# An adaLN transformer block on one core: another order of the opening, with the diagonals of silu(c) on ScalarE and all sixteen modulation columns on VectorE

## The chip, the cores and the metric

The kernel runs on one core of a Trainium2 chip. The metric is the device time of one execution in microseconds, given as the median of the runs. A core has five engines that run at the same time, each with its own in-order instruction stream: TensorE (PE in the profile, its weight loads PEld), VectorE (DVE), ScalarE (ACT), GpSimd (POOL) and SyncE (SP), which here issues the DMA transfers.

## The reference

A row `c` modulates a transformer block of two parts; everything is float32.

```python
mod = (silu(c) @ w_mod).reshape(1, 6, 1, 1024)      # sa, ca, ga, sb, cb, gb
h = layernorm(x) * (1 + ca) + sa                    # x: 2048 x 1024
x = x + ga * A(h)       # attention over 4 segments of 512 rows, 32 heads of 32,
                        # o = g * (memory of earlier segments) + (1 - g) * softmax attention, g = sigmoid(beta)
h = layernorm(x) * (1 + cb) + sb
x = x + gb * ((gelu(h @ w_gate) * (h @ w_up)) @ w_down)
```

Before any projection of the first segment of attention can start, the first two sixths of `mod` are needed (`sa` and `ca`): 2 x 1024 numbers, each a dot product of silu(c) with a column of `w_mod`.

## The kernel before, in words

The kernel has an opening, the attention stage and the feed-forward stage. The change touches the opening alone. In it the order of the instructions on each of the five engines is the order in which the program issues them: the string `OPENING` is read token by token, and each token issues a few instructions on one or several engines. An instruction at the head of an engine's queue that waits holds up all that was issued to that engine after it.

What the opening does, with the names of the profile:

- **Modulation columns.** A tile `wm` holds 128 columns of `w_mod`, turned so that each partition holds one column of 1024 numbers. `mod_col` (L175) multiplies it on VectorE by silu(c), repeated on all partitions in `scp`, and sums into one column of `modT`; for the scales (1 + ca) a second instruction adds one (L180). Block `kt` of the first segment needs the columns `C<kt>` (scale, number 8 + kt) and `c<kt>` (shift, number kt). The 16 tiles are loaded in eight pairs into four buffers of two halves (`wm_a` to `wm_d`), so that pairs 4 to 7 (tokens `p4` to `p7`) wait until the columns of pairs 0 to 3 are done. Two columns, `c6` and `C7`, are made on PE instead (`mod_mm`, L186): 16 matmuls each with one output column, and ScalarE copies the result (L187).
- **The silu row.** `scol` is silu(c) as 1024 numbers on 128 partitions. `row_parts` (L140) makes two tiles of diagonals on VectorE, one matmul with a tile of ones each (L146) puts the row on all partitions (`scp`), and ScalarE copies it to `scb` (L147), which the later columns use.
- **Normalization.** For each of four tiles of 128 rows: statistics on VectorE (L236 to L241; `s0` to `s3` for the first segment, `t0` to `t3` for the second), a power on GpSimd (L242), one small factor on VectorE (L1900) and two scalings by halves on ScalarE (L1903; `a0` to `a7`, `b0` to `b3`).
- **Blocks of h.** `norm_seg` (`n` for the first segment, `N` for the second): four transposes of x on PE (L350), which read one half of all four tiles; then ScalarE applies the columns (L357, `h`) and rounds to the high part (L363, `hha`), and GpSimd subtracts to the low part (L368, `hla`); in the second segment some of these two run on VectorE. The call that finishes block kt issues the transposes of block kt + 1.
- **Weights.** `rk`, `rq` and `rv` of the first head group are split in the same way: ScalarE rounds (`K`, first `q`, first `v`), and the rest is subtracted on VectorE (k, L194) or in four quarters on GpSimd (q and v, L204).
- **Projections.** `F` calls `first_part`: for each of eight blocks, twelve matmuls for keys and values (L590) and three for queries (L593); the ninth `F` copies keys and values out (`kn`, `vx`), the tenth turns the keys (`kT`), splits queries and keys (L469, L473, L443, L444) and sends them by DMA. `K` in the attention stage is the same for the second segment.
- **Beside these.** `selectors` makes a few small constant tiles; the gate shares `gall` (sigmoid of beta) and `omc` are made on ScalarE and VectorE (L131 to L133, L1888); two instructions on ScalarE spread a selector over 32 partitions of `ks` (L1906), all of this ahead of the first token. `x0` to `x3` load the second segment's x tiles into four buffers, three of which have held `rk`, `rq` and `rv`. `S` closes the opening's PSUM pool and opens the next.

Of the kernel before, what the change touches and what calls it, by code (L numbers as in the profile page):

```python
# [19 lines left out]
P = 128  # L20
D = 1024
# [15 lines left out]
def block_kernel(ctx: ExitStack, tc: tile.TileContext, x, c, wmod, wq, wkv, wo, beta, wg, wu, wd, out):  # L37
# [51 lines left out]
    def tmp_tile(name):  # L89
        return big.tile([P, L], F32, name=name, tag="tmp", bufs=4)  # L90
# [11 lines left out]
    def s_ps(name):  # L102
        return small[0].tile([P, L], F32, name=name, tag="s", bufs=small[2])
# [17 lines left out]
    ccol = cs([P, KT], "ccol")  # L121
    nc.sync.dma_start(ccol, c)
    bb = cs([P, H], "bb")
    nc.sync.dma_start(bb, bass.AP(tensor=beta.tensor, offset=beta.offset, ap=[[0, P], [1, H]]))
    def fetch(src, name):
        r = raw_tile("r" + name)
        nc.sync.dma_start(r, src)
# [7 lines left out]
    def row_parts(dst, cols, tmp, name):  # L135

        dgs = []
        for h in range(2):
            dg = tmp(f"{name}dg{h}")
            nc.vector.tensor_tensor(dg.rearrange("p (k m) -> p k m", m=P), ident.unsqueeze(1).to_broadcast([P, 4, P]),  # L140
                                    cols[:, 4 * h:4 * h + 4].unsqueeze(2).to_broadcast([P, 4, P]), op=ALU.mult)
            dgs.append(dg)
        yield
        for h in range(2):
            ps = scp[:, h * L:(h + 1) * L] if name == "sc" else s_ps(f"{name}{h}")
            nc.tensor.matmul(ps, ones, dgs[h], start=True, stop=True)  # L146
            nc.scalar.activation(dst[:, h * L:(h + 1) * L], ps, AF.Copy)  # L147
            yield
# [25 lines left out]
    def mod_col(r, w, behind=False):  # L174
# [3 lines left out]
            hold(i)  # L178
        if r // 8 in (1, 4):
            nc.vector.tensor_scalar_add(modT[:, r:r + 1], modT[:, r:r + 1], 1.0)  # L180

    def mod_mm(r, w):

        ps = s_ps(f"col{r}")
        for k in range(KT):
            nc.tensor.matmul(ps[:, :1], w[:, k * P:(k + 1) * P], scol[:, k:k + 1], start=(k == 0), stop=(k == KT - 1))  # L186
        nc.scalar.activation(modT[:, r:r + 1], ps[:, :1], AF.Identity, bias=1.0 if r // 8 == 1 else 0.0)  # L187

    def split_w(r, w, eng=nc.gpsimd):
        nc.scalar.activation(w[:, 0], r, AF.Copy)
# [698 lines left out]
    def feed_forward():  # L891
# [946 lines left out]
    AFTER = ('qo kt ek dq ea dk eb', 'kt qo ea eb dk dq ek')  # L1838
    HI_DVE = ((), (1, 5, 7))
    LO_DVE = ((), (0, 1, 5, 6, 7))  # L1840
    BY_PRODUCT = (6, 15)
    OPENING = (
        "s0 s1 a2 r r s2 a5 r q s3 a6 a4 a0 c0 C1 C0 K q n n a3 v p4 c1 q q C2 c3 c2 n p5 v C4 C3 F c5 n F q "
        "c4 F x0 v p6 p7 v a7 a1 C5 n v x1 t0 C6 n n F x2 c6 n x3 C7 c7 b0 t1 t2 F F n b1 F t3 F b2 S b3 F F "
        "N N N N N ")

    def opening():
        x0 = [[], []]
        for i in range(4):
            for h in range(2):  # L1850
                tag, bufs = ("pt0", 4) if h == 0 else ("sj", 3) if i < 3 else ("pq", 2)
                t = t2(f"x0_{i}_{h}", tag, bufs=bufs)
                nc.sync.dma_start(t, x[i * P:(i + 1) * P, h * L:(h + 1) * L])
                x0[h].append(t)
        free = [wsp_tile("wm_a"), wsp_tile("wm_b")] + [
            t2(f"wm_{q}", "qs", bufs=2, dt=F32R, shape=(P, 4, L)).rearrange("p (a b) t -> p a (b t)", a=2) for q in "cd"]
        spare = [f32(w[:, h]) for w in free for h in range(2)]
        got, raw0, x1t, x1h = {}, {}, [], [[], []]

        def pair(kt):  # L1860
            for r in (8 + kt, kt):
                got[r] = mod_load(r, spare[len(got) % 8])

        def x1_load(i):
            x1t.append(fetch(x[L + i * P:L + (i + 1) * P, :], f"x1_{i}"))

        pair(0)
        raw0[1] = fetch(wkv[0, 0], "k0")
        raw0[0] = fetch(wq[0], "q0")
        pair(1)  # L1870
        raw0[2] = fetch(wkv[0, 1], "v0")
        pair(2)
        pair(3)

        nc.vector.memset(ones, 1.0)
        nc.gpsimd.affine_select(ident, ones, pattern=[[-1, P]], compare_op=ALU.is_equal, fill=0.0,
                                base=0, channel_multiplier=1)
        nc.vector.memset(mask, 0.0)
        nc.gpsimd.affine_select(mask[:, L - P:], mask[:, L - P:], pattern=[[-1, P]],
                                compare_op=ALU.is_ge, fill=MASK, base=0, channel_multiplier=1)  # L1880
        nc.vector.memset(mhalf, -0.5)
        selectors()
        sigmoid(scol, ccol)
        nc.vector.tensor_mul(scol, scol, ccol)
        sigmoid(gall, bb)
        for j in range(4):
            q = slice(DH * j, DH * (j + 1))
            nc.vector.tensor_scalar(omc[q], gall[q].rearrange("p (g j) -> p g j", j=4)[:, :, j], -1.0, 1.0,  # L1888
                                    op0=ALU.mult, op1=ALU.add)
        row = row_parts(scb, scol, tmp_tile, "sc")  # L1890
        sc = {}

        def stats(s, i, halves):
            sc[s, i] = norm_stats([halves[h][i] for h in range(2)], f"a{s}_{i}") + ([],)

        def scaled(s, i, hs, halves):
            mv, rs, mr = sc[s, i]
            if not mr:
                mr.append(cs([P, 1], f"mr{s}_{i}", tag="mr", bufs=4))
                nc.vector.tensor_scalar(mr[0], mv[:, 0:1], rs, -1.0, op0=ALU.mult, op1=ALU.mult)  # L1900
            for h in hs:
                t = halves[h][i]
                nc.scalar.activation(t, t, AF.Identity, bias=mr[0], scale=rs)  # L1903

        for k in ks_t:
            nc.scalar.activation(k[96:128], selj[96:128].unsqueeze(2).to_broadcast([32, 4, L]), AF.Copy)  # L1906
        W[0] = [wsp_tile(f"w0_{i}") for i in range(3)]
        nseg = norm_seg(0, x0)
        low = [split_parts(raw0[i], W[0][i]) for i in range(3)]
        first, nseg1 = [], []  # L1910
        for u in OPENING.split():
            n = int(u[1:]) if u[1:] else 0
            if u[0] == "p":
                pair(n)
            elif u[0] == "x":
                x1_load(n)
                for h in range(2):
                    x1h[h].append(x1t[n][:, h * L:(h + 1) * L])
            elif u[0] == "r":
                next(row)  # L1920
            elif u[0] in "st":
                stats("st".index(u[0]), n, (x0, x1h)[u[0] == "t"])
            elif u[0] == "a":
                scaled(0, n // 2, (n % 2,), x0)
            elif u[0] == "b":
                scaled(1, n, (0, 1), x1h)
            elif u[0] == "C":
                (mod_mm if 8 + n in BY_PRODUCT else mod_col)(*got[8 + n])
            elif u[0] == "c":
                (mod_mm if n in BY_PRODUCT else mod_col)(*got[n])  # L1930
            elif u[0] == "K":
                split_w(raw0[1], W[0][1], nc.vector)
            elif u[0] in "qv":
                next(low["q.v".index(u[0])])
            elif u[0] == "n":
                next(nseg)
            elif u[0] == "N":
                if not nseg1:
                    nseg1.append(norm_seg(1, x1h))
                next(nseg1[0])  # L1940
            elif u[0] == "F":
                if not first:
                    first.append(first_part(0, 0, 0))
                next(first[0])
            elif u[0] == "S":
                s_all()
        return nseg1[0]
# [73 lines left out]
    def selectors():  # L2021
        pick = tmp_tile("pick")[:, :P].rearrange("p (j d) -> p j d", d=DH)
        nc.gpsimd.affine_select(pick, ones.rearrange("p (j d) -> p j d", d=DH), pattern=[[-1, 4], [-4, DH]],
                                compare_op=ALU.is_equal, fill=0.0, base=0, channel_multiplier=1)
        nc.vector.tensor_reduce(sel4, pick, axis=AX.X, op=ALU.add)
        nc.vector.tensor_copy(blk.rearrange("p (j e) -> p j e", e=DH), sel4.unsqueeze(2).to_broadcast([P, 4, DH]))
        eye = tmp_tile("eye")[:, :32].rearrange("p (j i l) -> p j i l", j=4, i=4)
        nc.gpsimd.affine_select(eye, ones[:, :32].rearrange("p (j i l) -> p j i l", j=4, i=4),
                                pattern=[[-8, 4], [-2, 4], [-1, 2]], compare_op=ALU.is_equal, fill=0.0,
                                base=-96, channel_multiplier=1)  # L2030
        nc.vector.tensor_reduce(selj, eye.rearrange("p j i l -> p j (i l)"), axis=AX.X, op=ALU.add)
        nc.vector.tensor_copy(seli, eye[:, 0, :, 0])
        for j in range(4):
            for part in range(2):
                if j or part:
                    nc.vector.tensor_add(seli, seli, eye[:, j, :, part])
# [58 lines left out]
```

## Time and profile before

| | |
|---|---|
| median of 3 runs | 2670.61 us (2669.91 to 2671.44) |
| profiled execution, its own time | 2672.39 us |
| its span in the profile | 2670.7 us |
| PE busy, share of the span | 2633.0 us, 99% |
| PE busy from 0 to 60 us | 41.8 us |
| mean granted clock of PE | 0.995 |

The span is the time from the first to the last recorded instruction; what lies around it is in the execution's own time. A line of the timeline gives start, duration, engine, source line, operation, output and inputs, and in brackets how long the engine had been idle before and what released it. A line of busy times by window gives the window, its length, then busy time and count of PE, PEld, DVE, ACT and POOL, the granted clock of PE (1.00 is full), the share of the transfer engines and GB/s. A line of the grouped view gives line, engine, operation, tiles, shapes and count, then busy time in us and mean ns of one, then idle time before them and its releasers.

### The profile page before, as it was taken

The numbers are of one execution on the slowest core, as the hardware profiler recorded it, in microseconds if no ns is written. First come the engines' busy times: TensorE is split into PE (matmuls) and PEld (weight loads), VectorE is DVE, ScalarE is ACT, GpSimd is POOL, SyncE is SP. The second block draws the span as 40 slices with busy tenths as digits, with TensorE's granted clock in tenths as the row PEclk, the third lists the DMA queues.
The fourth block names the chain that finished last, engine by engine and source line by source line (L and its number), as shares of the span: only waits on it lengthen the run. The fifth ranks groups of instructions, "written<-read, shape, count | busy, mean of one in ns | idle before, by whom it ended". The sixth has DMA issues, their size and how long they took to land.

```text
span 2670.7 us, 42495 instructions
## 1 busy us (share of the span) xinstructions
PE 2633.0 (99%) x13905; PEld 2193.0 (82%) x13905; DVE 1741.7 (65%) x3679; ACT 1383.3 (52%) x3163; POOL 1056.2 (40%) x1590
## 2 busy tenths in 40 slices
PE   7999999999999999999999999999999999999999
PEld 6888888888888788888787888788888888888887
DVE  6677666767667745787776556677767554574456
ACT  6787767767676734566564334433333333243323
POOL 4233333533334533345556665587868100000000
PEclk9999999999999999999999999999999999999999
DMA  7355454543544548588989778999999896885563
GB/s 263 108 151 152 118 147 127 147 127 109 157 115 127 166 166 288 162 291 295 329 310 334 264 277 294 343 364 364 362 365 359 305 325 221 279 294 194 186 210 121
DMA packets 286591, 622.04 MB, mean 233 GB/s; under 512 B 29344, under 2 KB 53920, under 8 KB 286368
## 3 DMA queue, kind: packets, MB, share of 16 engines
q1 hardware_dynamic: 286368, 619.32, 68.7%
q8 instruction: 109, 1.79, 0.3%
q14 instruction: 114, 0.93, 0.1%
HBM read 380.65 MB, written 188.22 MB: 213 GB/s over the span
## 4 chain that ended last, share of the span: by engine, by line
PE 93%; DMA 3%; DVE 2%; ACT 1%; issue 0%; POOL 0%; SPq 0%; DVEq 0%; ACTq 0%
PE y L1698 20%; PE f L1497 17%; PE kv L406 9%; PE pb L1274 8%; PE y L784 6%; PE q L412 6%; PE pa L1274 5%; PE pc L1274 5%; PE S L618 3%; PE T L706 3%; PE O L718 3%; PE kT L525 2%; PE vT L525 2%; PE num L674 1%; PE M L657 1%; PE kv L590 1%
## 5 line engine op out<-in xcount | busy, mean ns | idle before, releaser
L1698 PE MATMUL y<-B,L 128*128 128x512 f32 x2352 | 533.5, 389 | 0.0
L1698 PEld LDWEIGHTS y<-B,L 128*128 128x128 f32 x2352 | 441.5, 188 | 91.8 <-DVE L L934 0.3
L1497 PE MATMUL f<-A,B 128*128 128x512 f32 x2016 | 460.7, 390 | 3.8 <-DVE A L934 3.2
L1497 PEld LDWEIGHTS f<-A,B 128*128 128x128 f32 x2016 | 379.2, 188 | 85.2 <-DVE A L934 5.6
L622 ACT ACTIVATE sj<-sj,mm 128x384 f32<-128x384 f32 (+3 forms) x512 | 281.1, 552 | 40.1 <-DVE mm L620 39.6
L709 POOL TENSOR_SCALAR_AFFINE_SELECT pt<-pt 128x128 f32<-128x128 f32 x512 | 166.6, 347 | 332.5 <-ACT pt L708 324.5
L620 DVE CUSTOM_DVE_ANT_0 sj<-S,mask 128x384 f32<-128x384 f32 (+3 forms) x512 | 228.2, 488 | 97.4 <-PE S L618 69.4
L1274 PE MATMUL pb<-AA,BB 128*128 128x512 f32 x1008 | 248.5, 394 | 6.5 <-DMA AA<-hl_d 3.4
L708 ACT ACTIVATE pt<-T 128x256 f32<-128x256 f32 (+3 forms) x512 | 182.3, 444 | 133.1 <-PE T L706 126.7
L937 ACT ACTIVATE L<-X 128x512 fp32r<-128x512 f32 x168 | 105.8, 630 | 257.3 <-PE y L1698 168.1
L1274 PEld LDWEIGHTS pb<-AA,BB 128*128 128x128 f32 x1008 | 189.1, 189 | 50.8 <-ACT AA L1043 3.8
L934 DVE TENSOR_TENSOR L<-X,L 128x512 fp32r<-128x512 f32 x168 | 115.9, 691 | 145.4 <-ACT L L937 145.0
L397 POOL TENSOR_TENSOR w<-r,w 128x256 fp32r<-128x256 f32 x180 | 133.8, 773 | 141.7 <-ACT w L391 139.2
L1524 ACT ACTIVATE g<-f 128x512 f32<-128x512 f32 x56 | 33.5, 598 | 288.6 <-PE f L1497 288.6
L406 PE MATMUL kv<-w,hha 128*128 128x256 f32 x896 | 176.2, 287 | 2.2 <-DVE vx L424 2.2
L1274 PE MATMUL pc<-AA,BB 128*128 128x512 f32 x672 | 162.5, 390 | 0.4 <-DVE y L1300 0.4
L1274 PE MATMUL pa<-AA,BB 128*128 128x512 f32 x672 | 162.7, 390 | 0.0
L406 PEld LDWEIGHTS kv<-w,hha 128*128 128x128 f32 x896 | 146.0, 193 | 3.4 <-DVE vx L424 2.5
L1274 PEld LDWEIGHTS pc<-AA,BB 128*128 128x128 f32 x672 | 126.1, 188 | 26.9 <-DVE y L1300 0.8
L1274 PEld LDWEIGHTS pa<-AA,BB 128*128 128x128 f32 x672 | 126.0, 188 | 26.7 <-issue 0.5
L934 DVE TENSOR_TENSOR BB<-t_a,BB 128x512 fp32r<-128x512 f32 x98 | 79.5, 812 | 85.6 <-ACT BB L937 85.5
L934 POOL TENSOR_TENSOR t_a<-g,t_a 128x256 f32<-128x256 f32 x112 | 98.3, 897 | 76.2 <-DVE BB L934 71.4
(298 smaller groups left out, 5452.4 us busy)
## 6 DMA issues: line engine op xcount, KB each, us to landing
B<-wc_d SPq DMA_DIRECT2D x112, 512.0 KB, 3.8
cg<-st_d SPq DMA_DIRECT2D x168, 256.0 KB, 6.3
st_d<-x SPq DMA_DIRECT2D x112, 256.0 KB, 3.2
st_d<-y SPq DMA_DIRECT2D x112, 256.0 KB, 4.1
hid_d<-g SPq DMA_DIRECT2D x56, 512.0 KB, 5.9
wc_d<-T SPq DMA_DIRECT2D x56, 512.0 KB, 4.8
X<-hid_d SPq DMA_DIRECT2D x112, 256.0 KB, 4.9
wr<-gd_d SPq DMA_DIRECT2D x84, 256.0 KB, 4.2
```

The source lines that it names most:

```text
L397: nc.gpsimd.tensor_sub(w[:, 1, c], r[:, c], f32(w[:, 0, c]))
L406: nc.tensor.matmul(ps, b[:, sl], w[:, a], start=(kt == 0 and a == 0 and b is hi), stop=(kt == KT - 1 and a == 1), **kw)
L412: nc.tensor.matmul(ps, w[:, a], b, start=(kt == 0 and a == 0 and b is hi), stop=(kt == KT - 1 and a == 1), **kw)
L620: nc.vector.tensor_tensor_reduce(out=sj[:, :nv], in0=ps[:, :nv], in1=mask[:, L - nv:], scale=-1.0, scalar=3.4e38, op0=ALU.add, op1=ALU.min ...
L622: nc.scalar.activation(sj[:, :nv], sj[:, :nv], AF.Exp, bias=mm[:, j, i:i + 1], scale=-1.0, accum_out=ll[:, i, j:j + 1])
L708: nc.scalar.activation(pt, ps[:, nn - n:nn], AF.Exp)
L709: nc.gpsimd.affine_select(pt[:, :P], pt[:, :P], pattern=[[1, P]], compare_op=ALU.is_ge, fill=0.0, base=0, channel_multiplier=-1)
L784: nc.tensor.matmul(ps, b[:, i * P:(i + 1) * P], w[:, a, g % 2], start=(g == 0 and a == 0 and b is hi), stop=(g == G - 1 and a == 1))
L934: f(*xs)
L1274: nc.tensor.matmul(ps, w[:, a, at:at + P], A["a", i, r, k][b], start=(r in (1, 5) and k == a == b == 0), stop=(k == 1 and a == 1), skip_gr ...
L1497: nc.tensor.matmul(ps, B[fc, i][:, a, kt * P:(kt + 1) * P], A[p, i, kt][b], start=False, stop=(kt == 3 and a == 1), skip_group_check=True)
L1698: nc.tensor.matmul(banks[t], ops[k][:, y, t * P:(t + 1) * P], B[slots[k]][:, x], start=(i not in (2, 4, 3) and j == 0 and x == 0 and y == ...
```

## The change

- The silu row: the product scol = silu(c) is now made on VectorE ahead of `selectors`. Each of the two tiles of diagonals is made by four instructions on ScalarE (`D0`, `D1`), a scaled copy of the identity of 128x128 each. The two matmuls (`r0`, `r1`) follow directly, and the copies to `scb` are tokens of their own (`e0`, `e1`) further behind.
- All 16 columns are made by `mod_col` on VectorE, and in the order in which the pairs are loaded: C0 c0 C1 c1 to C7 c7. `mod_mm` is gone, and the host no longer turns two of the tiles for it.
- The two selector copies into `ks` are tokens (`k0`, `k1`) between blocks of the first segment.
- The gate shares are a token (`g`) behind the last column and the statistics of the second segment's first tile; the load of beta moves behind the eight x loads.
- The loads of the second segment's x (`x0` to `x3`) stand behind all the column pairs, and its statistics and scalings behind all the columns.
- Rounding k (`K`) and subtracting (`L`) are two tokens.

```diff
@@ -121,7 +121,7 @@
     ccol = cs([P, KT], "ccol")
     nc.sync.dma_start(ccol, c)
     bb = cs([P, H], "bb")
-    nc.sync.dma_start(bb, bass.AP(tensor=beta.tensor, offset=beta.offset, ap=[[0, P], [1, H]]))
+
     def fetch(src, name):
         r = raw_tile("r" + name)
         nc.sync.dma_start(r, src)
@@ -142,7 +142,7 @@
             dgs.append(dg)
         yield
         for h in range(2):
-            ps = scp[:, h * L:(h + 1) * L] if name == "sc" else s_ps(f"{name}{h}")
+            ps = s_ps(f"{name}{h}")
             nc.tensor.matmul(ps, ones, dgs[h], start=True, stop=True)
             nc.scalar.activation(dst[:, h * L:(h + 1) * L], ps, AF.Copy)
             yield
@@ -178,15 +178,6 @@
             hold(i)
         if r // 8 in (1, 4):
             nc.vector.tensor_scalar_add(modT[:, r:r + 1], modT[:, r:r + 1], 1.0)
-
-    def mod_mm(r, w):
-
-        ps = s_ps(f"col{r}")
-        for k in range(KT):
-            nc.tensor.matmul(ps[:, :1], w[:, k * P:(k + 1) * P], scol[:, k:k + 1], start=(k == 0), stop=(k == KT - 1))
-        nc.scalar.activation(modT[:, r:r + 1], ps[:, :1], AF.Identity, bias=1.0 if r // 8 == 1 else 0.0)
-
-
 
     def split_w(r, w, eng=nc.gpsimd):
         nc.scalar.activation(w[:, 0], r, AF.Copy)
@@ -1838,11 +1829,10 @@
     AFTER = ('qo kt ek dq ea dk eb', 'kt qo ea eb dk dq ek')
     HI_DVE = ((), (1, 5, 7))
     LO_DVE = ((), (0, 1, 5, 6, 7))
-    BY_PRODUCT = (6, 15)
     OPENING = (
-        "s0 s1 a2 r r s2 a5 r q s3 a6 a4 a0 c0 C1 C0 K q n n a3 v p4 c1 q q C2 c3 c2 n p5 v C4 C3 F c5 n F q "
-        "c4 F x0 v p6 p7 v a7 a1 C5 n v x1 t0 C6 n n F x2 c6 n x3 C7 c7 b0 t1 t2 F F n b1 F t3 F b2 S b3 F F "
-        "N N N N N ")
+        "D0 r0 D1 r1 s0 s1 a0 s2 e0 a2 s3 a4 C0 K e1 a6 c0 L n n q q F p4 C1 c1 k0 n F p5 a1 a3 C2 c2 q n F "
+        "p6 k1 C3 v c3 a5 a7 q v n F p7 C4 v c4 x0 n F C5 v c5 x1 n q F C6 v c6 x2 n F C7 x3 c7 n F t0 g t1 b0 t2 b1 F "
+        "t3 b2 S b3 F N N N N N ")
 
     def opening():
         x0 = [[], []]
@@ -1864,6 +1854,7 @@
         def x1_load(i):
             x1t.append(fetch(x[L + i * P:L + (i + 1) * P, :], f"x1_{i}"))
 
+        nc.sync.dma_start(bb, bass.AP(tensor=beta.tensor, offset=beta.offset, ap=[[0, P], [1, H]]))
         pair(0)
         raw0[1] = fetch(wkv[0, 0], "k0")
         raw0[0] = fetch(wq[0], "q0")
@@ -1879,15 +1870,18 @@
         nc.gpsimd.affine_select(mask[:, L - P:], mask[:, L - P:], pattern=[[-1, P]],
                                 compare_op=ALU.is_ge, fill=MASK, base=0, channel_multiplier=1)
         nc.vector.memset(mhalf, -0.5)
-        selectors()
         sigmoid(scol, ccol)
         nc.vector.tensor_mul(scol, scol, ccol)
-        sigmoid(gall, bb)
-        for j in range(4):
-            q = slice(DH * j, DH * (j + 1))
-            nc.vector.tensor_scalar(omc[q], gall[q].rearrange("p (g j) -> p g j", j=4)[:, :, j], -1.0, 1.0,
-                                    op0=ALU.mult, op1=ALU.add)
-        row = row_parts(scb, scol, tmp_tile, "sc")
+        selectors()
+
+        def shares():
+            sigmoid(gall, bb)
+            for j in range(4):
+                q = slice(DH * j, DH * (j + 1))
+                nc.vector.tensor_scalar(omc[q], gall[q].rearrange("p (g j) -> p g j", j=4)[:, :, j], -1.0, 1.0,
+                                        op0=ALU.mult, op1=ALU.add)
+
+        dgs = [tmp_tile(f"scdg{h}") for h in range(2)]
         sc = {}
 
         def stats(s, i, halves):
@@ -1902,8 +1896,6 @@
                 t = halves[h][i]
                 nc.scalar.activation(t, t, AF.Identity, bias=mr[0], scale=rs)
 
-        for k in ks_t:
-            nc.scalar.activation(k[96:128], selj[96:128].unsqueeze(2).to_broadcast([32, 4, L]), AF.Copy)
         W[0] = [wsp_tile(f"w0_{i}") for i in range(3)]
         nseg = norm_seg(0, x0)
         low = [split_parts(raw0[i], W[0][i]) for i in range(3)]
@@ -1916,8 +1908,18 @@
                 x1_load(n)
                 for h in range(2):
                     x1h[h].append(x1t[n][:, h * L:(h + 1) * L])
+            elif u[0] == "D":
+                for k in range(4):
+                    nc.scalar.activation(dgs[n][:, k * P:(k + 1) * P], ident, AF.Identity,
+                                         scale=scol[:, 4 * n + k:4 * n + k + 1])
             elif u[0] == "r":
-                next(row)
+                nc.tensor.matmul(scp[:, n * L:(n + 1) * L], ones, dgs[n], start=True, stop=True)
+            elif u[0] == "e":
+                nc.scalar.activation(scb[:, n * L:(n + 1) * L], scp[:, n * L:(n + 1) * L], AF.Copy)
+            elif u[0] == "k":
+                nc.scalar.activation(ks_t[n][96:128], selj[96:128].unsqueeze(2).to_broadcast([32, 4, L]), AF.Copy)
+            elif u[0] == "g":
+                shares()
             elif u[0] in "st":
                 stats("st".index(u[0]), n, (x0, x1h)[u[0] == "t"])
             elif u[0] == "a":
@@ -1925,11 +1927,13 @@
             elif u[0] == "b":
                 scaled(1, n, (0, 1), x1h)
             elif u[0] == "C":
-                (mod_mm if 8 + n in BY_PRODUCT else mod_col)(*got[8 + n])
+                mod_col(*got[8 + n])
             elif u[0] == "c":
-                (mod_mm if n in BY_PRODUCT else mod_col)(*got[n])
+                mod_col(*got[n])
             elif u[0] == "K":
-                split_w(raw0[1], W[0][1], nc.vector)
+                nc.scalar.activation(W[0][1][:, 0], raw0[1], AF.Copy)
+            elif u[0] == "L":
+                nc.vector.tensor_sub(W[0][1][:, 1], raw0[1], f32(W[0][1][:, 0]))
             elif u[0] in "qv":
                 next(low["q.v".index(u[0])])
             elif u[0] == "n":
@@ -2069,9 +2073,7 @@
     wkv = np.concatenate([by_head(A_wk).reshape(D, G, 1, P), np.asarray(A_wv).reshape(D, G, 1, P)], axis=2)
     wkv = wkv.reshape(2, 4, P, G, 2 * P).transpose(3, 0, 2, 1, 4)
     wo = np.asarray(A_wo).reshape(4, 2, P, 2, 512).transpose(3, 0, 2, 1, 4)
-    wmod = np.array(np.asarray(w_mod).T.reshape(48, P, D))
-    for r in (6, 15):
-        wmod[r] = np.asarray(w_mod)[:, r * P:(r + 1) * P].reshape(KT, P, P).transpose(1, 0, 2).reshape(P, D)
+    wmod = np.asarray(w_mod).T.reshape(48, P, D)
     arrays = {
         "x": np.asarray(A_x).reshape(T, D),
         "c": np.asarray(c).reshape(KT, P).T,
```

## The prediction

> **What bounds the kernel now.** I read the page first, then the busy time behind the opening, then the opening engine by engine in order of time.
>
> ```profile
> span 2670.7 us, 42495 instructions
> 60.00:2670.00 2610.00, 2591.24 (x13668) 2157.13 (x13666) 1698.90 (x3569) 1344.29 (x3108) 1032.56 (x1548) 1.00 0.69 232
> ```
>
> The second row gives length, then busy PE, PEld, DVE, ACT, POOL, clock, DMA. From 60 us on PE is busy for 2591.24 of 2610 us at full clock: what the opening saves or loses arrives at the end one to one, and nothing there can hide it. So the question is only when PE starts the continuous stretch that follows the opening. On PE:
>
> ```profile
> 20.09 2.79 PE L350 MATMUL tpa<-ident,x 128*128 128x128 f32 x12 [4.14 <-ACT x L1903]
> 22.71 1.22 PE L590 MATMUL kv<-w,hha 128*128 128x256 f32 x4
> 23.73 0.63 PE L593 MATMUL q<-hha,w 128*128 128x512 f32 x1
> 24.73 0.40 PE L593 MATMUL q<-hha,w 128*128 128x512 f32 x1
> ...
> 30.66 0.82 PE L590 MATMUL kv<-w,hha 128*128 128x256 f32 x4 [2.25 <-ACT hha L363]
> ...
> 35.66 0.72 PE L590 MATMUL kv<-w,hha 128*128 128x256 f32 x4
> ...
> 37.88 1.84 PE L186 MATMUL col<-scol,wm_c 128*128 128x1 f32 x16
> ...
> 40.05 2.21 PE L186 MATMUL col<-scol,wm_d 128*128 128x1 f32 x16
> 42.12 1.20 PE L590 MATMUL kv<-w,hha 128*128 128x256 f32 x4
> ...
> 46.11 1.05 PE L590 MATMUL kv<-w,hha 128*128 128x256 f32 x4
> ...
> 49.20 0.63 PE L590 MATMUL kv<-w,hha 128*128 128x256 f32 x4
> ...
> 51.33 0.64 PE L590 MATMUL kv<-w,hha 128*128 128x256 f32 x4
> ...
> 54.17 2.78 PE L350 MATMUL tpa<-ident,rx 128*128 128x128 f32 x24
> ...
> 68.51 3.21 PE L618 MATMUL S<-ks,qs 96*128 96x128 f32 x12
> ```
>
> Call the projection of one row block of the first segment F0 to F7 (12 matmuls of kv, 3 of q). From 49.20 to 51.33 one takes 2.13 us; from 42.12 to 46.11 one takes 3.99. The clock explains it:
>
> ```profile
> 32.00:34.00 2.00, 2.00 (x10) 1.90 (x10) 2.00 (x3) 1.32 (x3) 2.00 (x4) 0.50 0.96 346
> 44.00:46.00 2.00, 2.00 (x9) 1.90 (x9) 1.38 (x5) 1.97 (x4) 0.71 (x2) 0.50 0.00 0
> ```
>
> Half clock (0.50) follows the wait before 30.66 and the one-column products at 37.88 and 40.05. At 54.17 the second segment's 24 transposes begin; from there to the first scores at 68.51 PE runs 14.3 us without a gap. **The start of those transposes, 54.17, is what the change must beat**, together with the clock at that point.
>
> **The change, part by part.** *Silu row.* Diagonals on ScalarE: eight multiplications of 128x128 that the trace does not show.
>
> ```profile
> 4.72 0.17 DVE L1884 TENSOR_TENSOR scol<-scol,ccol 128x8 f32<-128x8 f32 x1
> 13.87 2.08 PE L146 MATMUL scp<-scdg,ones 128*128 128x512 f32 x2 [0.69 <-ACT scb L147]
> 45.12 4.33 ACT L1903 ACTIVATE rx<-rx,mr,rsa 128x512 f32<-128x512 f32 x6
> 53.18 0.66 ACT L423 ACTIVATE kn<-kv 128x256 f32<-128x256 f32 x2 [3.73 <-PE kv L590]
> 7.21 8.26 DMA rk<-wkv
> ```
>
> One lies between 0.28 (kn, half of 0.66 less the overlap) and 0.72 us (a sixth of 4.33, at 512); I take 0.35, nearest kn. Even from 4.9 and at 0.72 they end at 10.7, and the second product (2.08) at 12.8. In the new order ScalarE takes the copy of rk before the last first-half normalization (a6), and rk lands at 15.47. So either bound is hidden behind that load: the row can be some 6 us earlier and buys nothing by itself. The selectors' small operations only change places with it ahead of the first statistics.
>
> *To F0.* Copy of rk 15.5 to 16.5, half the silu row to 17.1, a6 to 17.9, four transposes (a third of 2.79) to 18.8. Then h, its high part, the copy of rq, on GpSimd the low part and a quarter of q's low part, all on queues that run in order:
>
> ```profile
> L357 ACT ACTIVATE h<-tpa,modT 128x512 f32<-128x512 f32 x13 | 9.8, 769 | 5.7 <-DVE modT L175 3.5 <-PE tpa L350 2.1
> L363 ACT ACTIVATE hha<-h 128x512 fp32r<-128x512 f32 x10 | 6.3, 631 | 0.3
> L201 ACT ACTIVATE w<-rq 128x1024 fp32r<-128x1024 f32 x1 | 1.1, 1056 | 0.2 <-DMA rq<-wq 0.2
> L1906 ACT ACTIVATE ks<-selj 32x2048 fp32r<-32x2048 f32 x2 | 3.7, 1896 | 0.0
> L368 POOL TENSOR_TENSOR hla<-h,hha 128x256 fp32r<-128x256 f32 x18 | 12.8, 732 | 21.0 <-ACT hha L363 21.0
> L204 POOL TENSOR_TENSOR w<-rq,w 128x256 fp32r<-128x256 f32 x4 | 2.9, 739 | 1.5 <-ACT w L201 1.5
> ```
>
> h to 19.7, high part to 20.3, low part (two of 0.73) to 21.8, quarter to 22.5: **F0 at 22.5, against 22.71 before**. q's first part used to lie under an idle time and now lies on the path.
>
> *Columns in the order of the loads.* Before, a column of the fourth pair stood ahead of one of the third:
>
> ```profile
> 26.70 1.23 DVE L175 CUSTOM_DVE_ANT_0 wm_d<-scp,wm_d 128x1024 f32<-128x1024 f32 x1 [2.07 <-DMA wm_d<-wmod]
> ```
>
> That wait held F2 back to 30.66, and it goes. Sixteen columns instead of fourteen cost VectorE two more at 1.23; from 26.7 the nine left (at 1.14 to 1.35) end at about 38 if loads keep up. They should: the transfer engines' share is 0.96 and more while columns are loaded (0.96 from 32 to 34 us, above), so beta's load behind the eight x loads, and the second segment's x behind the last two pairs on SP's queue, only reorder a full queue, in the columns' favour by one load of x. But ScalarE is late next. F0 and most of F1 run at half clock (F0 22.5 to 26.4); behind h2 and its high part (28.7) stand the second selector copy 1.9, v's copy 1.0, two normalizations 1.4, then h3 and its high part, 1.3: **F3 at 34.3, against 35.66**. With F0 and F1 at full clock the same ScalarE work ends at 32.9. The selector copies cost nothing before (they filled idle time ahead of the loads); here they are 3.7 us on this path.
>
> *F3 to the last block.* The products (1.84 and 2.21 of PE) and the half clock behind them go. PE's order is F3, transpose, F4, transpose, F5, transpose (of block 7): 3 x 2.13 and 3 x 0.45 (2.78/6) end at 42.05. Then h7 and its high part (0.15 latency, 0.77, 0.63): 43.6. Bounds: 42.2 from the earlier F3; 46.6 if 6 us of it run at half clock, as from 42 to 48 now. Before:
>
> ```profile
> 44.58 0.63 ACT L363 ACTIVATE hha<-h 128x512 fp32r<-128x512 f32 x1
> ```
>
> The high part of block 7 ended at 45.2, three of the second segment's four tiles (the six of 4.33, above) were normalized right behind it, and F7 ended near 53.6. Now F7 ends at about 46.5: seven us gained there.
>
> *The tail, where it is lost.* VectorE's order becomes: last column, statistics of tile 0, the shares, tiles 1 and 2, vx, tile 3. The shares begin with an exponential on ScalarE, which now **stands behind h7 and its high part**. VectorE waits from about 39.7 to 43.8 with everything queued behind it:
>
> ```profile
> 39.66 1.28 DVE L236 BATCH_NORM_STATS2 sta<-rx 128x6 f32<-128x512 f32 x2
> ...
> 41.36 1.28 DVE L236 BATCH_NORM_STATS2 sta<-rx 128x6 f32<-128x512 f32 x2
> 4.64 0.23 ACT L131 ACTIVATE gall<-bb 128x32 f32<-128x32 f32 x1 [1.94 <-DMA bb<-beta]
> 5.51 0.69 DVE L1888 TENSOR_SCALAR omc<-gall 32x8 f32<-32x8 f32 x4
> L424 DVE COPY vx<-kv 128x256 f32<-128x256 f32 x2 | 0.8, 420 | 6.1 <-ACT kn L423 6.1
> L1900 DVE TENSOR_SCALAR mr<-mva,rsa 128x1 f32<-128x1 f32 x8 | 1.6, 211 | 4.1 <-POOL rsa L242 4.1
> ```
>
> From the high part of block 7: exponential and shares 1.55 (4.64 to 6.20); three statistics of 1.70 (39.66 to 41.36), 5.1; vx 0.8; three small factors 0.4; then the last two tiles' scaling on ScalarE, 2.9 (four of six in 4.33). Sum 10.75. Every transpose of the second segment reads all four tiles, so **they start at 43.6 + 10.75 = 54.4, +0.2 against 54.17**.
>
> *The clock at the restart.* PE then has had nothing but kT for some 7 us. What a restart costs:
>
> ```profile
> 83.36 0.58 PE L406 MATMUL kv<-w,hha 128*128 128x256 f32 x1 [2.24 <-DVE vx L424]
> ...
> 89.07 0.46 PE L406 MATMUL kv<-w,hha 128*128 128x256 f32 x2
> ```
>
> There half clock lasts 5.7 us, a loss of 2.85; from 20.09 it lasts about 4.2 (a q matmul takes 0.63 at 23.73, 0.40 at 24.73), a loss of 2.1. I take 2.3, bounds 1.7 and 3.4. Before, 54.17 ran at full clock, so this is all new.
>
> **Sum:** +0.2 + 2.3 = **+2.5 us**. On the profiled execution's 2672.39 (span 2670.7 and 1.7 around it) that is 2674.9; it lies 1.8 above the median of the runs, so against the median of 2670.61 I forecast **2673.1**.
>
> [...]
>
> **The rivals.**
> *The half clock returns in the first segment too* (slower). If waits for ScalarE between F2 and F5 lower the clock as the one before 30.66 did, block 7 is ready at 46.6, the transposes start at 57.4 (+3.2), and with 2.85 for the restart it is +6.1: 2676.7. It decides once the waits add up to what 30.66 shows, 2.25 us; I find some 1 us ahead of F3, which speaks against.
> *The tail comes early* (faster side). If h7 follows the last column directly (38 + 1.4 = 39.4), the transposes start at 50.1 (-4.1), with 1.7 for the restart -2.4: 2668.2. It needs F5 to end by 37, and 22.5 + 6 x 2.13 + 5 x 0.45 = 37.5 allows that only without any wait or half clock.
> [...]
> *The last x tiles become the bound.* Their loads wait for q's and v's last quarters on GpSimd, now behind blocks 4 and 5, at about 41:
>
> ```profile
> rx<-x SPq DMA_DIRECT2D x4, 512.0 KB, 7.4
> ```
>
> At 7.4 they land at 48.4, while tile 3 is read at about 49.5. A load 2.6 later would add 1.5: 2674.6.
>
> **How the numbers follow.** Forecast 0.50, half clock in the first segment 0.16, early tail 0.20, transposes 0.06, late x 0.08. What a measurement can tell is 0.2%, 5.3 us. Faster by that would need the early tail and no restart cost and more: 0.08, for what I misread. Slower takes most of the first rival and the top of the forecast's bounds (46.6 and 3.4): 0.18. Within: 0.74. The forecast's own range is 2671 to 2676; with the rivals on both sides 2668 to 2677.5.
>
> **What would show it.** Right: F0 near 22.5, F3 near 34, F7 ending at 46 to 49; VectorE idle some 4 us before the shares' add, released by ScalarE's exponential; the second segment's transposes at 53.5 to 56, at 0.2 us apart. Wrong: statistics of the second segment running straight on behind the last column, transposes before 51, or a clock of 1.00 after them.

## The result, and the profile after

The changed kernel takes 2674.47 us in the median of 14 runs, the kernel before 2669.84 beside it: a ratio of 1.0020, 95% interval 1.0013 to 1.0028 (an estimate over the runs; the quotient of the two medians is 1.0017). It is slower by 4.6 us between the medians; the interval of the ratio corresponds to 3.5 to 7.5 us. Its profiled execution took 2673.36 us, 1.0 more than that of before (2672.39). Forecast were 2673.1 (+2.5), range 2668.0 to 2677.5; the median lies 0.17% above that of before, inside the margin of 0.2% that the prediction set, though the interval of the ratio lies above 1 and reaches beyond that margin.

The span, and the busy time behind the opening (columns as in the prediction):

```profile
span 2671.7 us, 42445 instructions
60.00:2671.00 2611.00, 2591.14 (x13685) 2157.08 (x13683) 1703.95 (x3570) 1345.23 (x3110) 1030.97 (x1549) 1.00 0.69 233
```

PE works 2591.14 us behind 60 us, against 2591.24 before: the work there is the same. PE through the opening of the changed kernel:

```profile
20.34 1.22 PE L581 MATMUL kv<-w,hha 128*128 128x256 f32 x4 [0.77 <-ACT hha L354]
...
33.19 0.74 PE L581 MATMUL kv<-w,hha 128*128 128x256 f32 x4 [1.00 <-ACT hha L354]
...
44.99 0.40 PE L584 MATMUL q<-hla,w 128*128 128x512 f32 x1
50.19 1.11 PE L431 MATMUL kT<-ident,kn 128*128 128x128 f32 x4 [4.80 <-ACT kn L414]
51.10 0.63 PE L341 MATMUL tpa<-ident,rx 128*128 128x128 f32 x2
53.57 0.47 PE L341 MATMUL tpa<-ident,rx 128*128 128x128 f32 x1 [1.84 <-ACT rx L1897]
54.98 4.36 PE L341 MATMUL tpa<-ident,rx 128*128 128x128 f32 x21 [0.94 <-ACT rx L1897]
59.10 0.72 PE L581 MATMUL kv<-w,hha 128*128 128x256 f32 x4
...
70.72 3.21 PE L609 MATMUL S<-ks,qs 96*128 96x128 f32 x12
```

The first segment's last projection ends at 45.4 instead of 53.6. Then PE sits still: 4.80 us for the copied keys, and two more waits, 1.84 and 0.94 us, for ScalarE's scaling of the second segment's tiles. The 21 transposes that need the last tile start at 54.98 (before: all 24 from 54.17), and they take 4.36 us instead of 2.4 (21 of 24 in 2.78). The first scores come at 70.72 instead of 68.51. What held the tail stands on VectorE and ScalarE:

```profile
42.81 0.70 DVE L132 TENSOR_SCALAR gall<-gall 128x32 f32<-128x32 f32 x1 [3.38 <-ACT gall L131]
...
44.73 1.29 DVE L227 BATCH_NORM_STATS2 sta<-rx 128x6 f32<-128x512 f32 x2
...
50.17 0.76 DVE L415 COPY vx<-kv 128x256 f32<-128x256 f32 x2 [1.85 <-ACT kn L414]
```

```profile
42.02 0.63 ACT L354 ACTIVATE hha<-h 128x512 fp32r<-128x512 f32 x1
42.56 0.21 ACT L131 ACTIVATE gall<-bb 128x32 f32<-128x32 f32 x1
...
49.78 0.63 ACT L414 ACTIVATE kn<-kv 128x256 f32<-128x256 f32 x2
52.70 2.93 ACT L1897 ACTIVATE rx<-rx,mr,rsa 128x512 f32<-128x512 f32 x4 [2.30 <-DVE mr L1894]
```

VectorE is idle for 3.38 us until the exponential of the shares, which ScalarE takes right behind block 7's high part. Later it is idle for another 1.85 us until ScalarE has copied the keys, which stand behind the scaling of tile 1. The clock in three windows of the wait and behind it:

```profile
52.00:54.00 2.00, 0.43 (x1) 0.18 (x1) 0.82 (x5) 1.29 (x2) 0.55 (x1) 0.50 0.00 0
56.00:58.00 2.00, 2.00 (x11) 2.00 (x10) 1.82 (x4) 1.97 (x5) 0.00 (x0) 0.50 0.27 104
58.00:60.00 2.00, 2.00 (x15) 1.96 (x14) 1.97 (x4) 1.97 (x4) 0.00 (x0) 0.80 1.10 245
```

### The profile page after: what moved, and what is told of

Read it like the earlier page. It is cut to its first block, busy times and chain, and to the rows that moved or that the text cites. A ratio compares the mean times of both kernels' runs of the same rounds, so it can differ in the third digit from the quotient of the medians.

```text
span 2671.7 us, 42445 instructions
## 1 busy us (share of the span) xinstructions
PE 2626.8 (98%) x13873; PEld 2186.1 (82%) x13873; DVE 1748.4 (65%) x3682; ACT 1384.9 (52%) x3169; POOL 1053.7 (39%) x1590
## 4 chain that ended last, share of the span: by engine, by line
PE 91%; DMA 4%; DVE 2%; ACT 1%; issue 1%; POOL 0%; SPq 0%; DVEq 0%; ACTq 0%; POOLq 0%
PE y L1689 19%; PE f L1488 16%; PE kv L397 10%; PE pb L1265 7%; PE y L775 6%; PE q L403 6%; PE pa L1265 5%; PE pc L1265 5%; PE S L609 3%; PE O L709 3%; PE T L697 3%; PE vT L516 2%; PE kT L516 1%; PE num L665 1%; PE M L648 1%; DMA wr<-gd_d 1%
```

## The experiments

My theory throughout: the in-order queues of the tail and the clock's fall set the start of the second segment, and what is won or lost there reaches the end. The rivals stand with each expectation.

**The shares early.** Token `g` moves to where ScalarE and VectorE are idle.

```diff
-  ... a4 C0 K e1 ...   n F t0 g t1 b0 ...
+  ... a4 C0 g K e1 ... n F t0 t1 b0 ...
```

> The changed kernel with one token moved: the gate shares stand right behind the first column C0 instead of behind the first statistics of the second segment. The exponential then finds ScalarE idle (it waits for rk from 13.6 to 15.9) and the shares find VectorE idle (15.1 to 17.5), and both landed before. My theory (VectorE is held 3.4 us by the exponential queued behind block 7's high part): VectorE runs straight on into tile 1, but the next wait is near: the power for tile 0 stands on GpSimd behind block 7's low part and ends at 44.7, so the factor of tile 0 holds VectorE until then; tile 2 to 46.4, the keys' copy behind tile 1's scaling to 48.7, tile 3 to 50.9, last transposes at 53.4 instead of 54.98: 1.6 us faster than the changed kernel, some 3 us slower than before. Rival (the second segment's last x tiles bind, landing near 43.6): also little, but VectorE waits on a DMA ahead of tiles 2 and 3. Rival (the lost time is not in the opening): transposes still at 55, no change of time.

Measured: 2672.32 us in the median against 2668.44 before, ratio 1.0015 (1.0006 to 1.0023). VectorE, GpSimd and PE:

```profile
45.29 0.21 DVE L1894 TENSOR_SCALAR mr<-mva,rsa 128x1 f32<-128x1 f32 x1 [4.60 <-POOL rsa L233]
```

```profile
43.32 1.43 POOL L359 TENSOR_TENSOR hla<-h,hha 128x256 fp32r<-128x256 f32 x2 [0.94 <-ACT hha L354]
44.71 1.07 POOL L233 TENSOR_TENSOR rsa<-rsa,mhalf 128x1 f32<-128x1 f32 x2
```

```profile
53.99 4.74 PE L341 MATMUL tpa<-ident,rx 128*128 128x128 f32 x21 [0.94 <-ACT rx L1897]
```

The wait for the shares is gone, and one of 4.60 us for the power stands in its place, because GpSimd takes it behind block 7's low part. The transposes win 1.0 us of an expected 1.6. They then take 4.74 us instead of 4.36, and the first scores, at 70.44, are only 0.28 earlier than in the changed kernel. VectorE waits for no DMA in this tail, so the loads of x do not bind here.

**The selector copies early.** `k0` and `k1` move into idle time of ScalarE ahead of the first blocks.

```diff
-  ... s0 s1 a0 ... a4 C0 ...       C1 c1 k0 n F ... p6 k1 C3 ...
+  ... s0 s1 k0 a0 ... a4 k1 C0 ... C1 c1 n F ...    p6 C3 ...
```

> The changed kernel with the two selector copies of 1.9 us moved to where ScalarE is idle: the first ahead of the first normalization (idle 5.9 to 9.3), the second ahead of the copy of rk (idle 13.6 to 15.9). My theory (ScalarE's queue sets blocks 1 to 3): block 3's high part at 30.4 instead of 33.1, block 7's at 39.5 instead of 42.65, where the columns (last one at 37.7) become the bound; the tail moves with it, last transposes at about 51.6, 3.3 us faster than the changed kernel, about 1 us slower than before. Rival (PE or the columns set the blocks already, the copies were covered): block 7 at 42 or later, no change of time.

Measured: 2671.28 us, ratio 1.0013 (1.0005 to 1.0022).

```profile
39.17 0.63 ACT L354 ACTIVATE hha<-h 128x512 fp32r<-128x512 f32 x1
```

```profile
38.67 1.29 DVE L227 BATCH_NORM_STATS2 sta<-rx 128x6 f32<-128x512 f32 x2 [1.04 <-DMA rx<-x]
```

```profile
52.12 4.74 PE L341 MATMUL tpa<-ident,rx 128*128 128x128 f32 x21 [0.94 <-ACT rx L1897]
```

Block 7's high part ends at 39.8 (expected 39.5) and the transposes start 2.9 us earlier. Block 3's high part ends at 30.3 instead of 33.1, so ScalarE's queue did set it, and the tail moves with it. VectorE no longer waits for the shares' exponential, which ends at 39.9; it waits 1.04 us for the load of the second segment's first x tile, ahead of that tile's statistics.

**Both moves.** The edits of both kernels above.

```diff
-  ... s0 s1 a0 ... a4 C0 K e1 ...         C1 c1 k0 n F ... p6 k1 C3 ... t0 g t1 ...
+  ... s0 s1 k0 a0 ... a4 k1 C0 g K e1 ... C1 c1 n F ...    p6 C3 ...    t0 t1 ...
```

> Both moves of the two kernels before this one. My theory: block 7's high part at 39.5; tile 0's factor at 41.7, tile 2 to 43.5, the keys' copy behind tile 1's scaling at 45.8, tile 3 to 48, last transposes at about 50.2: 4.7 us faster than the changed kernel, level with the kernel before. If the shares' place were worth its whole 3.4 us beside the other, it would be 6.5 us faster than the changed kernel.

Measured: 2669.03 us, ratio 1.0004 (0.9995 to 1.0013): no difference from before that can be measured.

```profile
51.08 4.74 PE L341 MATMUL tpa<-ident,rx 128*128 128x128 f32 x21 [0.93 <-ACT rx L1897]
...
67.57 3.21 PE L609 MATMUL S<-ks,qs 96*128 96x128 f32 x12
```

Two moves of small instructions take back what the change lost. The transposes start at 51.08, for an expected 50.2. The shares' place is worth 1.0 us beside the other move too, not 3.4: VectorE now waits 1.17 us for tile 0's power on GpSimd.

**Keeping PE at work through the gap.** Nine matmuls ahead of kT, their result unread (the trace records each as two).

```diff
+            elif u[0] == "W":
+                ps = s_ps("warm")
+                for k in range(9):
+                    nc.tensor.matmul(ps, ones, mask, start=True, stop=True)
-        "t3 b2 S b3 F N N N N N ")
+        "t3 b2 S b3 W F N N N N N ")
```

> The changed kernel with nine more matmuls of 128x512 (ones by the mask, result unread) on PE ahead of kT, so that PE works from 45 to about 53 instead of sitting idle. It measures the price of the restart at half clock. [...] Rival (half clock costs nothing that counts, or the matmuls delay kT): no change or up to 2 us slower.

Measured: 2671.67 us, ratio 1.0017 (1.0008 to 1.0025).

```profile
44.53 7.88 PE L1954 MATMUL warm<-mask,ones 128*128 128x512 f32 x18
...
54.28 1.64 PE L341 MATMUL tpa<-ident,rx 128*128 128x128 f32 x13 [1.08 <-ACT rx L1897]
56.79 1.09 PE L341 MATMUL tpa<-ident,rx 128*128 128x128 f32 x8 [0.87 <-DVE kl L435]
```

The clock stays at 1.00 in every window from 44 to 62 us, and the 21 transposes take 1.64 and 1.09 us; I had expected 2.3 instead of 4.36. From the last tile's first transpose to the first scores (69.42) it is 15.14 us instead of 15.74: 0.60 won, the 0.6 that I expected, since ScalarE is next: block 0's high part ends at 57.75 and the first projection starts at 57.80. I also expected a time 1 to 2 us below the changed kernel's. The medians against before are +3.2 here and +4.6 and +5.4 for the changed kernel in its two sets of runs; the intervals overlap.

**The tail in another order**, on top of both moves.

```diff
-  C7 x3 c7 n F t0 t1 b0 t2 b1 F t3 b2 S b3 F N N N N N
+  C7 x3 c7 t0 n F t1 b0 t2 F b1 t3 b2 S b3 F N N N N N
```

> The kernel with both early moves, and the tail in another order: statistics of the second segment's tile 0 ahead of block 7 (so that its power runs on GpSimd ahead of block 7's low part), then tile 1, tile 2, the copies of keys and values, tile 3. My theory (one in-order queue after another holds the tail): VectorE runs without a wait from 37.7 to 45.6, ScalarE's scalings then set the end: last tile scaled from 46.7, last transposes at 47.5 to 48 instead of 51.1; 3 us faster than the kernel with both moves, some 2 to 3 us faster than before. Rival (the last x tiles' loads are next): VectorE waits on a DMA ahead of tile 3 and the last transposes stay at 50 or later.

Measured: 2667.09 us against 2668.41, ratio 0.9992 (0.9984 to 1.0001).

```profile
47.93 4.74 PE L341 MATMUL tpa<-ident,rx 128*128 128x128 f32 x21 [1.08 <-ACT rx L1897]
...
64.70 3.21 PE L609 MATMUL S<-ks,qs 96*128 96x128 f32 x12
```

```profile
43.00 0.76 DVE L415 COPY vx<-kv 128x256 f32<-128x256 f32 x2 [0.16 <-ACT kn L414]
```

VectorE's wait for the copied keys falls from 1.85 to 0.16 us. The transposes start 3.15 us earlier than with both moves, as expected, the first scores 2.87; the median falls by 1.9, less than the 3 that were said, and against before the interval still includes 1.

**The tail with a tile on VectorE and PE at work**, and **the same without the matmuls**. Tile 3 is scaled by two multiply-adds on VectorE (`B3`); the first of the two kernels has three matmuls in the gap as well.

```diff
-  t3 b2 S b3 F N ...
+  t3 b2 S B3 W F N ...      (the second: t3 b2 S B3 F N ...)
   ...   (a small factor m for each row, from its mean and rs)
+                for h in range(2):
+                    nc.vector.tensor_scalar(x1h[h][n], x1h[h][n], rs, m, op0=ALU.mult, op1=ALU.add)
```

> The kernel with the tail's other order, with tile 3 of the second segment scaled on VectorE (two multiply-adds of 128x512) instead of ScalarE, and three more matmuls of 128x512 on PE ahead of kT, result unread, so that PE isn't idle from 43 to 46. My theory: last transposes at 47, at full clock; the transposes then take 2.6 instead of up to 5.2 us, the second segment starts 1.5 to 2.5 us earlier than with the reordered tail alone, first scores near 62.5, some 5 us faster than before. Rival (the clock's fall costs nothing once the gap is short): no difference from the reordered tail beyond 0.7.

> The reordered tail with tile 3 scaled on VectorE, without the three extra matmuls: it parts the two edits of the kernel that had both. My theory (the clock is most of that gain): last transposes at about 47.4 as there, but at half clock, 4.4 to 4.7 us instead of 1.64 and 1.09; first scores at 64 to 64.5 instead of 62.03; the time lies within 1 us of the reordered tail alone and 2 us above the kernel with the matmuls. Rival (VectorE's scaling made the gain): first scores below 63, time as with the matmuls.

Measured: with the matmuls 2664.53 us against 2668.41, ratio 0.9984 (0.9975 to 0.9993), 3.9 us faster than before where some 5 were expected, and inside the margin of 0.2%; without them 2666.33 against 2668.45, ratio 0.9995 (0.9986 to 1.0004). First with, then without:

```profile
47.42 1.64 PE L341 MATMUL tpa<-ident,rx 128*128 128x128 f32 x13 [0.23 <-DVE rx L1956]
...
62.03 3.21 PE L609 MATMUL S<-ks,qs 96*128 96x128 f32 x12
```

```profile
46.41 4.37 PE L341 MATMUL tpa<-ident,rx 128*128 128x128 f32 x22 [1.42 <-ACT rx L1897]
...
62.15 3.21 PE L609 MATMUL S<-ks,qs 96*128 96x128 f32 x12
```

The medians fall as my theory had it (0.8 below the reordered tail, 1.8 above the kernel with the matmuls), but the two intervals overlap, and the profile of the second kernel has its first scores at 62.15, where the rival put them: in that profile the clock was back soon (0.58 granted from 48 to 50 us, 1.00 from 50 on). That execution, 2663.10 us, is also the fastest of its eleven. How the gain divides between VectorE's scaling and the clock is therefore not settled.

**One part alone, on the kernel before: the columns in the order of their loads.**

```diff
-  ... C2 c3 c2 n p5 v C4 C3 F c5 ...
+  ... C2 c2 n p5 v C3 c3 C4 F c5 ...
```

> The kernel before with one part of the change alone: columns C2, c2, C3, c3 in the order of their loads, all else as it was. My theory (the wait of 2.25 us ahead of block 2 and the half clock behind it are real costs of the order): block 2's projection starts at about 28.4 instead of 30.66 and at full clock, the products of the two columns then wait for their loads (36.9 and 38.2) instead of PE; block 7 ends 2 to 3 us earlier and so does the first score: 2 to 3 us faster than before. Rival (PE's products and the second segment's scaling, which ends at 49.4, take it back): less than 1 us.

Measured: 2668.11 us against 2668.41, ratio 1.0000 (0.9991 to 1.0009): the rival's number, less than 1 us, came true.

```profile
34.79 1.92 PE L186 MATMUL col<-scol,wm_c 128*128 128x1 f32 x16 [0.98 <-ACT hha L363]
...
37.04 2.69 PE L186 MATMUL col<-scol,wm_d 128*128 128x1 f32 x16
...
51.21 2.78 PE L350 MATMUL tpa<-ident,rx 128*128 128x128 f32 x24
```

```profile
42.00:44.00 2.00, 2.00 (x9) 1.81 (x8) 1.85 (x7) 1.97 (x4) 1.70 (x3) 0.50 0.00 0
```

The wait ahead of block 2 is gone, the products run earlier, and in this profile the half clock falls behind them. Waits are still there: VectorE is busy for 2.56 of the 4 us from 28 to 32, and PE waits 0.98 us ahead of the products. The transposes start at 51.21, inside the spread of the kernel before, which the next runs show; which of these causes took the gain back is not shown.

**The kernel before, profiled twice more.** No edit.

> [...] The profile of before has half clock from 31.2 to 34.6 and from 41.4 to 48.2, and its own time is 2.5 us above the median of the runs. My theory: in this look the half clock falls elsewhere, first scores lie between 66 and 69 instead of 68.51, and the time differs in step; ratio 1.000. Rival: the opening repeats to 0.3 us and the spread comes from later stages.

> The kernel before, a third look. The first look had the first scores at 68.51 and a time of 2672.39, the second 64.75 and 2666.67. [...] Rival: the first look was the rule, near 68.5.

Measured: 2668.53 us in the median of the runs of the second profile, ratio 0.9998 (0.9989 to 1.0006); the profiled executions took 2666.67 and 2667.99. PE in the second profile, then in the third:

```profile
29.99 0.74 PE L590 MATMUL kv<-w,hha 128*128 128x256 f32 x4 [2.19 <-ACT hha L363]
...
50.42 2.78 PE L350 MATMUL tpa<-ident,rx 128*128 128x128 f32 x24
...
64.75 3.21 PE L618 MATMUL S<-ks,qs 96*128 96x128 f32 x12
```

```profile
29.39 0.74 PE L590 MATMUL kv<-w,hha 128*128 128x256 f32 x4 [1.41 <-ACT hha L363]
...
48.30 2.78 PE L350 MATMUL tpa<-ident,rx 128*128 128x128 f32 x24
...
62.64 3.21 PE L618 MATMUL S<-ks,qs 96*128 96x128 f32 x12
```

The window from 40 to 42 us, the same two profiles:

```profile
40.00:42.00 2.00, 2.00 (x10) 1.90 (x9) 1.82 (x6) 2.00 (x3) 1.80 (x3) 0.50 0.02 8
```

```profile
40.00:42.00 2.00, 2.00 (x16) 1.87 (x15) 1.82 (x6) 1.97 (x4) 1.67 (x3) 1.00 0.03 10
```

The same program starts the second segment at 54.17, 50.42 or 48.30. Of these 5.9 us, 1.3 are there before block 2: it starts at 30.66, 29.99 and 29.39, and by the same steps ScalarE's wait for that block's column on VectorE ends (29.17, 28.50, 27.90). In the first profile VectorE's own wait, for a half of `wm_d`, ends at 26.70. From block 2 to the transposes it is 23.51, 20.43 and 18.91 us, and there the half clock differs: some 10 us of it in the first profile, some 3 in the second, none in the third. The profile that the prediction was made from was the latest of the three.

Neither expectation held in its range. The half clock did fall elsewhere and the ratio is 1.000, but 64.75 lies below 66 to 69, and 62.64 below the 64.5 to 68.6 that I expected of the third profile. The time that is not in the first scores is 2603.88, 2601.92 and 2605.35 us in the three profiled executions, not the expected 2602 to 2604, and over the thirteen of this page from 2600.0 to 2605.4. So the rival of the first expectation holds in part: later stages vary by some microseconds as well, and the time of one execution does not follow its opening alone.

**The changed kernel, profiled again.** No edit.

> The changed kernel once more, to see how far its opening moves between looks and to have its ratio beside the others of this call. My theory: VectorE's, ScalarE's and GpSimd's times repeat to 0.5 us (shares' add near 42.8, last tile's transposes near 55), what differs is the half clock behind them; first scores between 70 and 72.5; ratio to before 1.001 to 1.003. Rival (the tail's times themselves differ by microseconds from run to run): transposes more than 1 us away from 55.

Measured: 2673.81 us against 2668.45, ratio 1.0020 (1.0011 to 1.0028); profiled execution 2673.24.

```profile
54.38 4.38 PE L341 MATMUL tpa<-ident,rx 128*128 128x128 f32 x21 [0.93 <-ACT rx L1897]
...
70.12 3.20 PE L609 MATMUL S<-ks,qs 96*128 96x128 f32 x12
```

The changed opening repeats to 0.6 us between the two profiles. Its gap of 4.8 us is followed by a clock of 0.50 in both, from 50 to 58 us.

## Why the prediction was right, and where it was off

- *Where it is decided.* Right in the main. Busy time behind 60 us is the same, and the medians move with the start of the second segment. Single executions also differ behind it, by some microseconds.
- *The silu row buys nothing by itself.* Consistent with the trace, not tried alone. The eight diagonals took 2.44 us, 0.31 each, where 0.35 was assumed. The row is in `scp` by about 8 us and the first column waits for its load at 13.52 anyway. A wait that I had not named came with it: the second column waits 2.45 us, until 17.52, for the row's copy on ScalarE, which stands behind the copy of rk. It cost block 0 at most the 0.7 us for which its h waits.
- *F0 at 22.5.* Measured 20.34. The high part was forecast right:

```profile
19.65 0.63 ACT L354 ACTIVATE hha<-h 128x512 fp32r<-128x512 f32 x1
```

  It ended at 20.28, for 20.3 said. The low part and q's quarter were put on the path ahead of F0 wrongly: F0's first matmuls read high parts alone. The profile of before had it already, with PE at 22.71 and GpSimd's low part only from 22.73. The error is 2.2 us there and 1.1 at F3 (33.19 for 34.3), since ScalarE works from 18.84 to 34.47 without a wait and sets the blocks between; the run with the selector copies moved shows that its queue sets block 3.
- *F3 to block 7: 43.6.* Measured 42.65, at full clock. F7 ends at 45.4, said were 46.5. No row shows the 0.15 us that was put between block 7's transposes and its h: here they end at 41.13 and h starts at 41.21. The stage itself was sized right (9.5 us from F3, 9.3 said); it came early because F3 did.
- *VectorE waits for the shares from 39.7 to 43.8.* Measured 39.4 to 42.8, released by ScalarE's exponential, as said.
- *The tail, 10.75 us.* This term was mis-sized: from 42.65 to the end of the last scaling at 55.63 it took 12.98. Missing were the 1.85 us in which VectorE waits for the copy of the keys behind ScalarE's scaling of tile 1, and 0.5 in the shares' add. The transposes need only the first half of the last tile, 0.7 us before that end, and block 7 was 1 us early; so 54.98 stands against 54.4.
- *The restart, 2.3 us.* The 21 transposes took 4.36 instead of 2.4 us, near 2.0; that ScalarE's h would be next and leave 0.6 of it was not in the sum. Of the two stretches that the 2.3 came from, the one at 83.36 shows in the granted clock too (0.50 from 83 to 89 us). The one from 20.09 was read from durations alone; the clock recorded there is 1.00 from 18 to 30 us. The price is not the same everywhere: with the shares early, the selector copies early and both, the transposes took 4.74 us, and from them to the first scores it was 16.45 to 16.49 us, some 1.3 more than the 15.14 at full clock.
- *The sum.* +2.5 was forecast on the pair of profiles, and the first scores moved by +2.21. That these are near is in part luck: the transposes start 0.81 us later (+0.2 was said), and from them to the first scores it is 15.74 instead of 14.34 us, 1.40 more (2.3 was said), so that two errors nearly cancel. The median moved by 4.6. The step that failed is what these were held against: I took 54.17 and 68.51 as what the kernel before does, and half clock behind the products as its rule. Its three profiles have first scores at 68.51, 64.75 and 62.64, mean 65.3, the changed kernel's two 70.72 and 70.12, mean 70.4. The difference, 5.1, agrees with the medians, as far as three and two profiles can say it. The prediction noted that its execution lay 1.8 us above the median, and did not ask what that said of the opening. That execution, 2672.39 us, was slower than each of the 14 runs beside the result (up to 2671.44). Had the 1.8 us been put down to the opening, the same sum would have read +4.3.
- *The rivals.* No half clock in the first segment from F3 on, in either profile, though the waits ahead of F3 add up to 2.44 us (1.06, 0.38 and 1.00), more than the 2.25 at which I let it return; the clock is 1.00 from 26 to 48 us. The early tail did not come; no VectorE wait on the last x tiles. The 0.06 for transposes was a chance that they leave the clock low; in the changed kernel it came back during 21 of them (below).

## What to carry to other kernels

When an order is rewritten by hand, follow each small instruction through the queue of its own engine: an exponential of 0.2 us behind a late block cost a wait of 3.4 us, and once it was moved, a power of 0.55 us on another engine held the same chain for 4.6. Work that fills idle time at one place is on the path at another: moving two copies was worth 2.9 us at the transposes here. And before a single profile serves as the base of a sum of a few microseconds, take two or three: here the base itself moved by 5.9 us.

## What the runs showed of the hardware

- The clock after a stretch of little PE work is not the same from run to run. The products with one output column were followed by half clock for some 7 us, some 3 us and not at all, in three profiles of one program (0.50 from 42 to 48 us; 0.50 from 40 to 42 and 0.72 from 42 to 44; 1.00 throughout). A wait of 2.25 us ahead of block 2 was followed by it (0.50 from 32 to 34), one of 2.19 us in the next profile was not (1.00 from 30 to 38), nor was one of 1.41 (1.00 from 28 to 62). A gap of 4.80 us brought it in the first profile of the changed kernel (0.79 from 48 to 49, 0.50 from there to 58), one of 4.82 in the second (0.51 from 48 to 50). What decides where it falls is not shown.
- The changed kernel's 21 transposes started at 54.98 with no other matmul among them, and the next matmul, at 59.10, already ran at full speed (0.72 us for four). The granted clock was 0.50 up to 58 us, 0.59 from 58 to 59 and 1.00 from there on. So in this profile the clock came back while PE ran nothing but transposes of 128x128 in float32. The other profile of this kernel repeats it (transposes from 54.38, a clock of 0.50 up to 58 and 0.94 from 58 to 60, four matmuls in 0.71 us at 58.52). With the shares early it came later: the 21 took 4.74 us from 53.99, and the clock was 0.67 from 58 to 60.
- The shares' add of 128x32 took 0.70 us instead of 0.18 before. It ran from 42.81 to 43.51, and GpSimd's first subtraction of two from 42.73 to about 43.47. The add of before, then GpSimd's two subtractions:

```profile
4.91 0.18 DVE L132 TENSOR_SCALAR gall<-gall 128x32 f32<-128x32 f32 x1
```

```profile
42.73 1.43 POOL L359 TENSOR_TENSOR hla<-h,hha 128x256 fp32r<-128x256 f32 x2 [0.92 <-ACT hha L354]
```

  GpSimd did nothing from 4 to 6 us, around the add of before. In the second profile of the changed kernel and in the kernel with PE kept at work, the add again took 0.70 us, from 42.20 and 42.11, with two subtractions on GpSimd from 42.13 and 42.04. With the selector copies early it took 0.28 us, from 40.38, beside two subtractions from 39.88. In all four it ended within 0.1 us of the first subtraction's end, taken as half of the two. No run was made to test it, and the cause is not shown.
